# A fused attention, soft mixture and two-layer kernel: four kinds of vector work of a head pair take other places in its 18 half steps

## The chip, the cores and the metric

The kernel runs on one core of a Trainium2 chip. The metric is the device time of one execution in microseconds (us). Three executions of the kernel before took 703.08, 703.65 and 704.19 us, median 703.65.

## What is computed

The reference has three stages in a row, all in float32:

```python
q_pool = q.reshape(B, H, S // 2, 2, D).mean(axis=3)      # B 4, H 8, S 1152, D 64
attn = softmax(q_pool @ k^T / sqrt(D))
x = (attn @ v)  ->  (B * S / 2, H * D) = (2304, 512)
logits = x @ phi;  dispatch softmax over tokens, 8 experts of 4 slots, relu, combine softmax over slots
h = x @ w_in;  g = h (h >= 1), 0 (h <= -1), (h + 1)^2 / 4 between;  out = g @ w_out
```

Only the first stage, the attention, is touched by the change. It takes about the first 408 us.

## The kernel before

**Pairs, steps and half steps.** The 32 heads are handled as 16 pairs P = 0 to 15, two heads of one batch at a time, so a batch is four pairs. A pair is 9 steps, one for each chunk of 128 keys, and a step has two halves, one for each head. A half step is called a slot here: slot s of a pair is step s // 2, half s % 2, and runs from 0 to 17. Slot 18 is slot 0 of the next pair. The loop over all steps is at L694, and for each half it emits, in this order: one half of a maximum for the pair that comes 11 steps later (L711), the scores of this chunk (`st`, L373), the products with V of the step before (`pv`, L404), and then whatever the tables have put into this slot (`slot`, L619).

**The maximum.** The row maximum that the softmax subtracts is taken as max(a, b) = relu(a - b) + b over the two halves of the keys. In an even slot the matmuls multiply the queries with the difference of the key halves (`KD`) and ScalarE takes the relu (L332). In an odd slot the matmuls multiply with the first half of the keys and one VectorE instruction adds, and reduces to a maximum (L335, called the reduce here).

**The three score buffers.** All these matmul results and the scores share one pool of three PSUM tiles (L70, L72), taken in turn: maximum of slot s, scores of slot s, maximum of slot s + 1, scores of slot s + 1 and so on. With three tiles the scores of slot s + 1 take the tile that the maximum of slot s had. So the scores of an even slot can start only when the reduce of the odd slot before has ended, and the scores of an odd slot only when the relu of the even slot before has ended.

**Sums of exponentials.** ScalarE takes the exponential of each score tile (L388). VectorE adds the tiles of chunks 1 to 7 to a running sum for each head (`es_add`, L391; table `ADD`, entries (slot, chunk, head)). TensorE reduces the sums at the start of the next pair (`es_sum`, L396), where it also transposes the output of an earlier pair and takes its logits (`t_x`, L435).

**Preparing a pair.** Some 24 steps before a pair starts, its keys and queries are loaded (`load_k` L236, `load_q` L244). ScalarE then makes the high parts of the keys in float16 (`prep_khi`, L262, one for each head), VectorE the low parts (`prep_klo`, L267), both go through a DMA transpose (`xpose_k`, L276), and VectorE takes the difference of the key halves (`k_diff`, L313). For the queries VectorE adds neighbours (`prep_qp`, L282), ScalarE makes the high part (`prep_qhi`, L288), a DMA transposes it (`xpose_q1`, L299), VectorE makes the low part (`prep_qlo`, L295). The buffers of the raw keys, the raw queries and the high and low parts (`kf`, `qf`, `kn`) are there once, so each load waits for the last use by the pair before.

**Where each piece goes.** `plan` (L567) puts all this into slots, from the tables `PREP` and `KDS` (L37, L38; half steps relative to the start of the pair; -37 is 19 steps before it, second half) and `ADD` (L32). One table of `PREP` is for pair 2, the other for pairs 3 to 15. In a slot the pieces come in the order of pairs, and behind them the weight conversion: `cv_abs` on ScalarE and four VectorE steps (`cv_step`, L207), one weight block in each pair, from the table `CVS` (L26; first the slot of `cv_abs`, then of the four steps). VectorE, ScalarE and the queue that issues all DMAs (SP) each run their instructions in the order in which they were emitted.

A pair P is prepared while pair P - 2 runs, so what the tables set for pair 10 is seen in the slots of pair 8. In the middle of the attention pair 8 starts at 226.87 us and pair 6 at 177.21 us, counted at their first scores.

Of the kernel before, what the change touches and what calls it, by code (L numbers as in the profile page):

```python
# [22 lines left out]
MB = {1: 3, 2: 10, 3: 20}  # L23
DU = (3, 4, 5)

CVS = (10, 12, 17, 18, 19), (8, 9, 10, 11, 12)  # L26
CVL = 1
P1G = 0, 1, 1, 2, 2, 3, 4, 5, 6
TML = (3, 0, 4), (6, 1, 4)
WPH = 6  # L30

ADD = (((4, 1, 0), (4, 1, 1), (6, 2, 0), (8, 2, 1), (9, 3, 0), (8, 3, 1), (11, 4, 0),  # L32
        (10, 4, 1), (11, 5, 0), (14, 5, 1), (16, 6, 0), (14, 6, 1), (17, 7, 0), (17, 7, 1)),
       tuple((2 * c + h + 1 + (c < 8), c, h) for c in range(1, 9) for h in range(2)))
ADD += tuple((16, *x[1:]) if x == (17, 7, 0) else x for x in ADD[0]),

PREP = (-20, (-36, -35), (-34, -33), (-33, -32), -33, -32, -31, -30), (-24, (-42, -40), (-37, -37), (-35, -34), -38, -37, -35, -31)  # L37
KDS = -26, -19  # L38


@with_exitstack
def fused_kernel(ctx: ExitStack, tc: tile.TileContext, q, k, v, phi, w1, w2, w_in, w_out, out):
# [521 lines left out]
    def at(g, slot, f, *a):  # L564
        sched.setdefault((g, slot), []).append((f, a))

    def plan(P):  # L567
        b = NK * P
        if P > 1:
            lk, hk, lok, xk, aq, hq_, xq, loq = PREP[P > 2]  # L570

            def sl(x, f, *a):
                at(b + x // 2, x % 2, f, *a)

            for h in range(2):
                at(b + lk, h, (load_k2, load_q)[h], P)
                sl(hk[h], prep_khi, P, h)
                sl(lok[h], prep_klo, P, h)
                sl(xk[h], xpose_k, P, h)
                sl(KDS[h], k_diff, P, h)  # L580
            sl(aq, prep_qp, P)
            sl(hq_, prep_qhi, P)
            sl(xq, xpose_q1, P)
            sl(loq, prep_qlo, P)
            sl(xq + (6 if P > 2 else 4), dup_q1, P)
        if P > 0:
            at(b - 8, 1, load_v, P)
            at(b - 4, 0, s2_fill, P, 0, 5)
            at(b, 0, s2_fill, P, 5, NK)
        last = P == NP - 1  # L590
        for s, *a in ADD[2 if P in (5, 9, 13) else last]:
            at(b + s // 2, s % 2, es_add, P, *a)
        if not last:
            pre.setdefault((b + 9, 0), []).append((es_sum, P))
        q_ = P // HPB
        if last:
            at(b + 9, 0, t_raw, P, 0)
            at(b + 9, 1, t_raw, P, 1)
            for f, *a in ((es_sum, P), (t_sum, P, 0), (t_sum, P, 1), (t_fin, P), (t_x, P, True), (warm, WARM[0]), (t_last, P),
                          (lg_mx, q_), (lg_tr, q_), (warm, WARM[5]), (lg_max, q_), (lg_rep, q_), (p_old, q_), (warm, WARM[1]), (lg_exp, q_),  # L600
                          (p_mm, q_), (warm, WARM[6]), (p_add, q_)):
                at(b + 10, 0, f, *a)
            return
        g0 = b + (11 if P == NP - 2 else 18)
        pre.setdefault((g0, 0), []).insert(0, (t_x, P))
        for i in range(2):
            at(g0, 0, t_ev, P, i)
        at(b + 10, 0, t_fin, P)
        for c, h, t in TML:
            at(g0 + c // 2, c % 2, t_mul, P, h, t)  # L610
        at(g0 + 3, 1, lg_add, P)
        for h in range(2):
            at(b + 9, h, t_raw, P, h)
            at(b + 9, h, t_sum, P, h)
        if P % HPB == HPB - 1:
            for s, f, *a in ((10, lg_mx), (12, lg_tr), (12, lg_max), (14, lg_rep), (14, lg_exp), (16, p_mm), (16, p_add)):
                late.setdefault((g0 + s // 2, s % 2), []).append((f, (q_, *a)))
# [11 lines left out]
    with tc.manual_schedule():  # L629
# [51 lines left out]
        for P in range(NP):  # L681
            plan(P)
        g1_ = NK * (NP - 1)
        for n in range(16):
            ab, *st_ = [2 * NK * n + x for x in CVS[n // 15]]
            at(*divmod(ab, 2), cv_abs, n)
# [7 lines left out]
        for g in range(-LEAD, nsteps + 1):  # L694
            mx = [divmod(g + LEAD, NK)] if not NK <= g + LEAD < 2 * NK else []
            mx += [(1, t) for t in range(NK) if P1G[t] == g]
            P, c = divmod(g, NK)
# [489 lines left out]
```

## Time and profile before

| | |
|---|---|
| median of 3 runs | 703.65 us |
| the profiled execution | 703.25 us, span 701.4 us |
| TensorE (PE) busy | 690.0 us, 98% |
| VectorE (DVE) busy | 556.4 us, 79%; slices of 99% in most of the attention |
| ScalarE (ACT) busy | 497.5 us, 71% |
| granted TensorE clock | 1.00 throughout |
| mean DMA share of q1 | 61.9% over the span |

The profile is one execution, and times in it are counted from the start of its span. The busy share of TensorE counts a matmul from its start to a modelled end, and matmuls overlap, so how far TensorE is held up is read from the starts of its matmuls instead. A timeline row gives start, duration, engine, line, operation, tiles and count, and in brackets idle time before it.

### The profile page before, as it was taken

To read this page: it belongs to the slowest core of one execution; us is meant where nothing else is said; L and a number is where in the kernel's file an instruction comes from. 1 tells how busy PE (TensorE), PEld (TensorE's weight loads), DVE (VectorE), ACT (ScalarE), POOL (GpSimd) and SP (SyncE) were. 2 spreads that over 40 slices of the span, in tenths; PEclk is the share of its full clock that TensorE was granted. 3 is DMA by queue.
4 is the path that set the end of the run, shared out by engine and by line. 5 is a ranking of instruction groups with operands and counts; after the bars stand their busy time and mean duration, and the time that the engine had idled before them with its cause. 6 is when DMAs were issued, how large, how long until landed. Compare 5 with 4: busy or idle time off the path is not lost.

```text
span 701.4 us, 18916 instructions
## 1 busy us (share of the span) xinstructions
PE 690.0 (98%) x7639; PEld 548.1 (78%) x7639; DVE 556.4 (79%) x1094; ACT 497.5 (71%) x884; POOL 139.4 (20%) x123
## 2 busy tenths in 40 slices
PE   8899999999999999999999999999999999999997
PEld 8678878887888887888887876348888888888886
DVE  5699999999899999999998867327678888796542
ACT  4688888788788887788886865118787686677640
POOL 5100110110110110110010020113444353345340
PEclk9999999999999999999999999999999999999999
DMA  9978789988888987987885567993002212200222
GB/s 210 232 159 217 166 214 232 229 174 237 206 171 243 228 165 215 227 173 212 227 202 162 166 220 279 413 383 111 1 31 91 71 50 76 77 30 1 90 90 91
DMA packets 133766, 118.70 MB, mean 169 GB/s; under 512 B 81392, under 2 KB 103920, under 8 KB 131632
## 3 DMA queue, kind: packets, MB, share of 16 engines
q1 hardware_dynamic: 133680, 117.50, 61.9%
q8 instruction: 60, 0.98, 0.6%
q14 instruction: 26, 0.21, 0.1%
HBM read 82.90 MB, written 8.91 MB: 131 GB/s over the span
## 4 chain that ended last, share of the span: by engine, by line
PE 91%; DVE 4%; DMA 2%; ACT 1%; issue 1%; SPq 0%; POOL 0%; DVEq 0%; POOLq 0%; ACTq 0%
PE po L1023 27%; PE st L383 20%; PE acc L408 19%; PE mx L325 10%; PE h L953 2%; PE acc L401 2%; PE h L766 2%; DVE RW L335 2%; PE fill L344 2%; PE ty L448 1%; DMA Wst<-cv_dr 1%; PE tx L442 1%; PE s2o L823 1%; PE pb L537 1%; DVE es L394 0%
## 5 line engine op out<-in xcount | busy, mean ns | idle before, releaser
L388 ACT ACTIVATE e<-st 128x576 f32<-128x576 f32 x288 | 187.5, 652 | 53.0 <-PE st L383 51.9
L408 PE MATMUL acc<-e,vf 128*64 128x288 f32 x1152 | 198.4, 406 | 0.2 <-ACT e L388 0.2
L394 DVE TENSOR_TENSOR es<-es,e 128x576 f32<-128x576 f32 x194 | 144.4, 758 | 5.7 <-ACT e L388 0.4
L383 PE MATMUL st<-q,K 128*64 128x288 f16 x1152 | 129.5, 287 | 2.0 <-ACT e L388 0.5
L383 PE MATMUL st<-q,S 128*64 128x288 f16 x1152 | 129.5, 286 | 0.0
L335 DVE CUSTOM_DVE_ANT_0 RW<-mx,RW 128x576 f32<-128x576 f32 x144 | 108.4, 755 | 23.8 <-ACT e L388 14.2
L325 PEld LDWEIGHTS <-q 128*64 128x64 f16 x1152 | 74.3, 110 | 55.6 <-issue 8.4
L1023 PE MATMUL po<-whi,ghi 128*128 128x512 f32 x280 | 109.3, 390 | 0.0
L1023 PE MATMUL po<-wlo,ghi 128*128 128x512 f32 x280 | 109.0, 389 | 0.0
L1023 PE MATMUL po<-whi,glo 128*128 128x512 f32 x280 | 108.6, 388 | 0.0
L992 POOL TENSOR_TENSOR glo<-r,ghi 128x1024 fp32r<-128x1024 f32 x34 | 81.9, 2408 | 112.6 <-DVE r L980 66.3
L332 ACT ACTIVATE RW<-mx 128x576 f32<-128x576 f32 x144 | 93.4, 650 | 14.2 <-PE mx L325 9.5
L408 PEld LDWEIGHTS acc<-e,vf 128*64 128x64 f32 x1152 | 84.2, 137 | 2.1 <-ACT e L388 1.2
L383 PEld LDWEIGHTS <-K 128*64 128x64 f16 x1152 | 75.8, 109 | 11.7 <-issue 7.8
L489 POOL TENSOR_TENSOR xl<-xl,ss 128x320 f32<-128x320 f32 x15 | 12.5, 830 | 363.3 <-DVE wst L214 192.4
L383 PEld LDWEIGHTS <-S 128*64 128x64 f16 x1152 | 76.3, 110 | 1.0
L1035 DVE TENSOR_TENSOR pa<-po,pa 128x512 f32<-128x512 f32 (+1 forms) x54 | 36.8, 682 | 38.5 <-PE po L1023 38.4
L325 PE MATMUL mx<-KD,q 128*64 128x288 f16 x576 | 62.4, 287 | 3.1 <-DMA q<-qn 1.4
L325 PE MATMUL mx<-K,q 128*64 128x288 f16 x576 | 62.7, 288 | 0.1
L1023 PEld LDWEIGHTS po<-whi,glo 128*128 128x128 f32 x280 | 52.6, 188 | 11.4 <-POOL glo L992 0.3
L1023 PEld LDWEIGHTS po<-whi,ghi 128*128 128x128 f32 x280 | 52.7, 188 | 10.4 <-issue 0.4
L1023 PEld LDWEIGHTS po<-wlo,ghi 128*128 128x128 f32 x280 | 52.7, 188 | 9.5
(205 smaller groups left out, 900.6 us busy)
## 6 DMA issues: line engine op xcount, KB each, us to landing
w<-in_moe_w_dram SPq DMA_DIRECT2D x76, 256.0 KB, 4.0
w<-in_moe_w_dram SPq DMA_DIRECT2D x12, 1024.0 KB, 10.8
vf<-in_v_dram SPq DMA_DIRECT2D x16, 576.0 KB, 5.9
kf<-in_k_dram SPq DMA_DIRECT2D x30, 288.0 KB, 6.9
f<-in_moe_w_in_dram SPq DMA_DIRECT2D x16, 512.0 KB, 5.2
f<-in_moe_w_out_dram SPq DMA_DIRECT2D x16, 512.0 KB, 3.5
qf<-in_q_dram SPq DMA_DIRECT2D x30, 256.0 KB, 7.7
out_dram<-pa SPq DMA_DIRECT2D x17, 256.0 KB, 2.0
```

The lines of the kernel that those rows point to most:

```text
L325: nc.tensor.matmul(ps[p0:p1, i, 0:HQ], lhsT=q1[P][:, t, p0:p1], rhs=kk[:, i * HQ:(i + 1) * HQ], start=True, stop=True)
L332: nc.scalar.activation(out=RW[:, t % 2], in_=ps[:, :, 0:HQ], func=AF.Relu)
L335: nc.vector.tensor_tensor_reduce(out=r, in0=ps[:, :, 0:HQ], in1=r, scale=1.0, scalar=-3.0e38, op0=ALU.add, op1=ALU.max, accum_out=mp[P][:, ...
L344: nc.tensor.matmul(fl[0][:, 0:128], lhsT=ident, rhs=ident, start=True, stop=True)
L383: nc.tensor.matmul(ps[c0:c0 + 64, i, 0:HQ], lhsT=kk[:, ci, c0:c0 + 64], rhs=f[:, sl[i]], start=first, stop=not first)
L388: nc.scalar.activation(out=e, in_=ps[:, :, 0:HQ], func=AF.Exp, scale=ESC)
L394: nc.vector.tensor_tensor(out=Es[P, h], in0=E[P, 0, h] if c == 1 else Es[P, h], in1=E[P, c, h], op=ALU.add)
L401: nc.tensor.matmul(acc[P, h][32 * r:32 * r + 32, HQ:HQ + SW], lhsT=ones.to_broadcast([128, 32]), rhs=a, start=False, stop=False, skip_grou ...
L408: nc.tensor.matmul(acc[P, i][h * 64:(h + 1) * 64, 0:HQ], lhsT=vt[P][:, h, c, :], rhs=E[P, c, h][:, i, :], start=(c == 0), stop=(c == NK - ...
L992: nc.gpsimd.tensor_tensor(out=glo[k], in0=r, in1=ghi[k].bitcast(F32), op=ALU.subtract)
L1023: nc.tensor.matmul(ps, lhsT=a, rhs=b, start=st_, stop=sp)
L1035: nc.vector.tensor_tensor(out=t, in0=po, in1=t, op=ALU.add)
```

## The change

For pairs 3 to 15 the loads of keys and queries move one step later (-24 to -23), the two high parts one half step later, the two low parts from one slot (-37) to two (-33 and -30), their transposes from -35 and -34 to -32 and -29, the addition of queries one half step earlier (-38 to -39), and the second key difference from -19 to -16. In all pairs but the last, four additions move: (chunk 5, head 0) from slot 11 to 12, (5, 1) from 14 to 13, (6, 0) from 16 to 14, (7, 0) from 17 to 16. The last already stood at 16 in pairs 5, 9 and 13, whose own table goes away. The second conversion step moves from slot 17 to 16. No instruction is added or removed.

```diff
-CVS = (10, 12, 17, 18, 19), (8, 9, 10, 11, 12)
+CVS = (10, 12, 16, 18, 19), (8, 9, 10, 11, 12)
 ADD = (((4, 1, 0), (4, 1, 1), (6, 2, 0), (8, 2, 1), (9, 3, 0), (8, 3, 1), (11, 4, 0),
-        (10, 4, 1), (11, 5, 0), (14, 5, 1), (16, 6, 0), (14, 6, 1), (17, 7, 0), (17, 7, 1)),
+        (10, 4, 1), (12, 5, 0), (13, 5, 1), (14, 6, 0), (14, 6, 1), (16, 7, 0), (17, 7, 1)),
        tuple((2 * c + h + 1 + (c < 8), c, h) for c in range(1, 9) for h in range(2)))
-ADD += tuple((16, *x[1:]) if x == (17, 7, 0) else x for x in ADD[0]),
-PREP = (...), (-24, (-42, -40), (-37, -37), (-35, -34), -38, -37, -35, -31)
-KDS = -26, -19
+PREP = (...), (-23, (-41, -39), (-33, -30), (-32, -29), -39, -37, -35, -31)
+KDS = (-26, -19), (-26, -16)
...
-                sl(KDS[h], k_diff, P, h)
+                sl(KDS[P > 2][h], k_diff, P, h)
...
-        for s, *a in ADD[2 if P in (5, 9, 13) else last]:
+        for s, *a in ADD[last]:
```

The entries of `PREP` are: loads (a step), high parts, low parts, key transposes (each for two heads), query addition, query high part, query transpose, query low part.

Seen in the slots of a running pair, the vector work stands so (the reduce of each odd slot comes first in it):

| slots | before | after |
|---|---|---|
| 1, 2 | conversion step 4; end of the pair before (L431, L433) | the same, key difference 1 |
| 3, 4 | two additions | low part, two additions |
| 5, 6 | query low part, addition | query low part, addition, low part |
| 7, 8 | two additions | the same |
| 9, 10 | two additions, key difference 0 | the same |
| 11, 12 | two additions, conversion step 1 | the same order |
| 13, 14 | L348, two additions | L348, three additions |
| 15, 16 | addition, query addition | query addition, addition, conversion step 2 |
| 17, 18 | two additions, key difference 1, two low parts, conversion step 2, L463, conversion step 3 | addition, L463, conversion step 3 |

## Rows read from the trace of the kernel before

**Rows 1.** The page: busy time of each engine, and the chain that ended last.

```profile
PE 690.0 (98%) x7639; PEld 548.1 (78%) x7639; DVE 556.4 (79%) x1094; ACT 497.5 (71%) x884; POOL 139.4 (20%) x123
...
PE 91%; DVE 4%; DMA 2%; ACT 1%; issue 1%; SPq 0%; POOL 0%; DVEq 0%; POOLq 0%; ACTq 0%
```

**Rows 2.** Busy time by stretch: pairs 6 and 8, first score to first score (length first).

```profile
177.21:201.98 24.77, 24.77 (x366) 20.47 (x367) 22.44 (x46) 20.63 (x38) 2.54 (x3) 1.00 0.88 192
...
226.87:251.76 24.89, 24.79 (x370) 20.53 (x367) 23.30 (x47) 20.84 (x39) 2.12 (x3) 1.00 0.90 212
```

**Rows 3.** Timeline of TensorE, pair 8: slots 1 to 3, then slots 13 and 14.

```profile
230.71 0.41 PE L383 MATMUL st<-q,K 128*64 128x288 f16 x4
...
232.19 0.44 PE L383 MATMUL st<-q,K 128*64 128x288 f16 x4
...
233.41 0.44 PE L383 MATMUL st<-q,K 128*64 128x288 f16 x4
...
245.61 0.44 PE L383 MATMUL st<-q,K 128*64 128x288 f16 x4
...
246.88 0.44 PE L383 MATMUL st<-q,K 128*64 128x288 f16 x4
```

**Rows 4.** Timeline of VectorE from slot 17 of pair 7 to slot 1 of pair 8.

```profile
225.99 0.76 DVE L335 CUSTOM_DVE_ANT_0 RW<-mx,RW 128x576 f32<-128x576 f32 x1 [0.31 <-ACT e L388]
...
226.67 1.42 DVE L394 TENSOR_TENSOR es<-es,e 128x576 f32<-128x576 f32 x2
228.01 0.45 DVE L315 TENSOR_TENSOR KD<-K 128x576 f16<-128x576 f16 x1
228.38 1.42 DVE L273 SCALAR_TENSOR_TENSOR kn<-kf,kn 128x576 f16<-128x576 f32 x2
229.72 0.42 DVE L214 TENSOR_SCALAR wst<-wst 128x512 int32<-128x512 int32 x1
230.05 0.68 DVE L463 TENSOR_TENSOR xl<-tx,ss 128x512 f32<-128x512 f32 x1
...
231.39 0.75 DVE L335 CUSTOM_DVE_ANT_0 RW<-mx,RW 128x576 f32<-128x576 f32 x1
```

**Rows 5.** Timeline of VectorE in slots 13 to 15 of pair 8.

```profile
246.06 0.75 DVE L335 CUSTOM_DVE_ANT_0 RW<-mx,RW 128x576 f32<-128x576 f32 x1
...
246.94 1.61 DVE L394 TENSOR_TENSOR es<-es,e 128x576 f32<-128x576 f32 x2
248.47 0.75 DVE L335 CUSTOM_DVE_ANT_0 RW<-mx,RW 128x576 f32<-128x576 f32 x1
```

**Rows 6.** Timelines of VectorE, TensorE and ScalarE in slots 1 to 3 of pair 6.

```profile
181.37 0.76 DVE L335 CUSTOM_DVE_ANT_0 RW<-mx,RW 128x576 f32<-128x576 f32 x1 [0.35 <-ACT es L427]
...
183.81 0.76 DVE L335 CUSTOM_DVE_ANT_0 RW<-mx,RW 128x576 f32<-128x576 f32 x1
...
182.27 0.41 PE L383 MATMUL st<-q,K 128*64 128x288 f16 x4
...
183.64 0.44 PE L383 MATMUL st<-q,K 128*64 128x288 f16 x4
...
182.92 0.66 ACT L332 ACTIVATE RW<-mx 128x576 f32<-128x576 f32 x1
```

**Rows 7.** Loads of keys and queries: times to landing, and who waited (L242, L253).

```profile
DMA to landing us min/median/max: 2.9/6.9/8.5
...
DMA to landing us min/median/max: 3.3/5.8/6.9
```

**Rows 8.** Timeline of SyncE: the issues of a key transpose and of loads, pair 8.

```profile
232.69 1.53 SPq L279 DMA_TRANSPOSE K<-kn  x1
...
235.94 0.90 SPq L242 DMA_DIRECT2D kf<-in_k_dram  x2
```

**Rows 9.** Line 220 (conversion step 4), the two groups, and GpSimd in pair 8.

```profile
L220 DVE SCALAR_TENSOR_TENSOR wst<-f,wst x16: 684/931/942, 55.8 to 423.6; 128x512 int32<-128x512 int32 x16
...
230.99 1.45 POOL L496 TENSOR_TENSOR xT<-xT,xl 128x160 f32<-128x160 f32 x2
```

More of the change, by code (lines that the diff above doesn't have):

```diff
@@ L32 @@
 ADD = (((4, 1, 0), (4, 1, 1), (6, 2, 0), (8, 2, 1), (9, 3, 0), (8, 3, 1), (11, 4, 0),
-        (10, 4, 1), (11, 5, 0), (14, 5, 1), (16, 6, 0), (14, 6, 1), (17, 7, 0), (17, 7, 1)),
+        (10, 4, 1), (12, 5, 0), (13, 5, 1), (14, 6, 0), (14, 6, 1), (16, 7, 0), (17, 7, 1)),
        tuple((2 * c + h + 1 + (c < 8), c, h) for c in range(1, 9) for h in range(2)))
-ADD += tuple((16, *x[1:]) if x == (17, 7, 0) else x for x in ADD[0]),
-PREP = (-20, (-36, -35), (-34, -33), (-33, -32), -33, -32, -31, -30), (-24, (-42, -40), (-37, -37), (-35, -34), -38, -37, -35, -31)
-KDS = -26, -19
+PREP = (-20, (-36, -35), (-34, -33), (-33, -32), -33, -32, -31, -30), (-23, (-41, -39), (-33, -30), (-32, -29), -39, -37, -35, -31)
+KDS = (-26, -19), (-26, -16)
 @with_exitstack
```

## The prediction

> **What bounds the kernel now.** I read the page first: TensorE is busy 98% of the span, and 91% of the chain that ended last is TensorE's [rows 1]. That says little yet, since a matmul that waits for the next to start still counts. So I went to the starts of the scores. In the middle of the attention one slot follows the other after 1.22 us, a step after 2.44 us: 232.19 to 233.41 [rows 3]. Slot 1 of pair 8 takes 1.48 us (230.71 to 232.19), 0.26 more, and slot 13 takes 1.27 (245.61 to 246.88), 0.05 more [rows 3]. Nothing else in that pair is late, so of its 24.89 us [rows 2] some 24.58 are TensorE's own work and 0.31 are lost. That is all a better order could give back in a plain pair.
>
> Who makes TensorE late is seen in VectorE's timeline. The scores of slot 2 start at 232.19, right when the reduce of slot 1 (231.39, 0.75 long) ends at 232.14 [rows 3, 4]: they take its PSUM tile. On time, the reduce would have begun 0.36 us earlier, at 231.03 (0.59 us behind its matmuls, as in the slots where VectorE had idled before; slot 1 of pair 6 is such a one, idle 0.35 [rows 6]). So 0.36 late cost 0.26; in slot 13 0.11 late cost 0.05. A reduce may thus be about 0.08 us late for nothing, and everything over that is TensorE's loss. After the loss the whole pace has shifted, and only those 0.08 are carried on. This is the rule of my sum: **each step has one deadline, and between two reduces there is 2.44 us of VectorE time.**
>
> **Prices.** From start to start, a reduce takes 0.68 (225.99 to 226.67), an addition 0.67 (two in 1.34, 226.67 to 228.01), the key difference 0.37, a low part 0.67 (two in 1.34), conversion step 2 0.33, all in [rows 4]. Two additions to the same sum in a row take 1.53 (246.94 to 248.47 [rows 5]), as the second waits for the first. A query addition and a query low part have the same shape as an addition, and I take 0.67 for each too. From reduce 13 to the first addition after it 0.88 pass (246.06 to 246.94 [rows 5]), L348 included.
>
> **What the change takes away.** At the end of a pair VectorE has two additions, a key difference, two low parts and the conversion step, 226.67 to 230.05, before L463 can start [rows 4]. One addition, the difference, both low parts and the step leave: 0.67 + 0.37 + 1.34 + 0.33 = 2.71. The 0.36 of slot 1 is gone. But slot 0 is also the one place where VectorE has room: TensorE takes 3.84 us for it (226.87 [rows 2] to 230.71 [rows 3]), 2.62 more than for another, on transposes, logits and sums. From reduce 17 to reduce 1 there are 2.44 + 2.62 = 5.06 us, and what is left to do is 0.68 + 0.67 + 1.34 (L463 and conversion step 3, 230.05 to 231.39 [rows 4]). L463 needs the transposes, so nothing moves up: VectorE will idle 2.37 us there.
>
> **What it adds, window by window** (a window runs from one reduce to the next; 2.44 is free, 0.08 grace, used up once):
> - Slots 1 to 3. Pair 6 is what a pair looks like whose slot 1 is on time: its slot 2 takes 1.37 (182.27 to 183.64 [rows 6]), 0.15 lost to ScalarE, whose relu (182.92 to 183.58 [rows 6]) comes late behind the last sums of the pair before. That stays. Its reduces stand 2.44 apart (181.37, 183.81 [rows 6]), with nothing left. The key difference adds 0.37: reduce 3 at 184.18, its end at 184.94, scores 0.14 late beyond the 0.15. Loss 0.29.
> - Slots 3 to 5: reduce, low part, two additions: 0.68 + 3 x 0.67 = 2.69, 0.25 over. Loss 0.25.
> - Slots 5 to 7: reduce, query low part, addition, low part: 2.69. Loss 0.25.
> - Slots 7 to 11: unchanged, and 0.2 of room in the first; the grace is back.
> - Slots 11 to 13: (5, 0) moves a slot, yet VectorE's order is the same. The 0.05 stays.
> - Slots 13 to 15: 0.88 and three additions, 2.01, make 2.89 (they alternate between the sums, so none waits): 0.45 over, and 0.01 from the window before. Loss 0.46. The high parts now stand in odd slots, ahead of a relu instead of behind an exponential. That makes the relu of slots 14 and 16 some 0.4 late, as in slot 2 of pair 6, worth 0.15; but TensorE already waits there for the reduce, so I add nothing. With that cover gone it is 0.15 twice.
> - Slots 15 to 17: 0.68 + 0.67 + 0.67 + 0.33 = 2.35, fits.
>
> The sum is 0.29 + 0.25 + 0.25 + 0.05 + 0.46 = 1.30 a pair in place of 0.31: **+0.99**. VectorE's total agrees: it was busy 23.30 of 24.89 us [rows 2], the work is nearly the same, and 2.37 us of idleness at the boundary with some 0.2 in slots 7 to 9 make a pair of 25.9.
>
> **Over all pairs.** Plain ones (2, 3, 4, 7, 8, 11, 12, like pair 8): 7 x 0.99 = 6.9. Pairs 6 and 10, which lose 0.19 now (24.77 [rows 2]): 2 x 1.11 = 2.2. Pairs 5, 9, 13, in which a batch is closed and which already had (7, 0) at 16: the first windows +0.05, 0.25 and 0.25, slots 13 to 15 +0.40, so 3 x 0.95 = 2.9. Pair 14 prepares nothing and has no reduce after slot 13: +0.1. Pair 0 has only slots 13 to 15: +0.4. Pair 1 lacks the moved difference: 0.25 + 0.25 + 0.46 - 0.31, +0.6. Together 13.1 us. The profiled execution took 703.25 us, 0.40 under the median; on the median the sum is 703.65 + 13.1 = **716.8 us**.
>
> **The queue of transfers.** SP issues in order. By the windows above, on pair 8's clock, reduce 1 stands at 231.03, reduce 3 at 233.84, reduce 5 at 236.53, reduce 13 near 246.6 and reduce 15 near 249.5. The second key transpose now waits for a low part that ends at 236.53 + 0.68 + 3 x 0.67 + 0.1, 239.3, and takes 1.53 to issue [rows 8]; behind it stand the copy of the queries, the loads of the next keys (0.45 each [rows 8]) and queries, and the copy of the scores' second operand. So keys are issued near 241.3 in place of 235.94 [rows 8], and the last queries near 244.5 (an estimate, with 0.5 to 0.6 an issue). Landing takes 2.9 to 8.5 us for keys and 3.3 to 6.9 for the last queries [rows 7], depending on what is ahead. Keys are needed near 247.5 (high part, behind the exponential of slot 13) and land between 244.2 and 249.8; queries are needed at 249.5 + 0.68, 250.2 (addition, slot 15), and land between 247.8 and 251.4. The wait is therefore 0 to 1.2 for queries, 0 to 2.3 for keys. I take 0 for both, because the large values of today come from loads issued in one burst behind others, and the new order spreads them; at the medians, 248.2 and 250.3, the waits would be 0.7 and 0.1, and I keep that as a rival. The cover of the moved loads is these 5 to 6 us. The copy behind them (needed in slot 0 of the next pair) has 7. GpSimd's queue is passed by nothing that moves.
>
> **A rule weighed against a row.** Conversion step 4 takes 0.68 at the least and 0.93 at the median; it is long where GpSimd's additions, until 232.44, run beside it [rows 9]. So company costs 0.25, and it does so already. After the change the step starts at 231.71 in place of 232.06, deeper in that company; the moved difference and low part start after 233, behind it. I add nothing. The Trainium skill, "SBUF — State Buffer", section "Who interferes with whom", says that a VectorE instruction with two SBUF inputs and a GpSimd instruction that reads SBUF exclude each other and that the loser blocks fully. The row's 0.25 is less than that; rival 4 is what full blocking would do.
>
> **Rivals.**
> 1. **Late loads on top** (chance 0.14). A wait for keys or queries of 0.7 to 1.2 comes in 13 preparing pairs and little of it is covered: 716.8 + 13 x 0.7 to 13 x 1.1, 726 to 731. For it: today's landing times. Against it: the burst ahead of the loads is gone.
> 2. **Faster** (0.06). The stall in slot 1 goes and the full windows are absorbed, because a reduce may be 0.45 late for nothing in place of 0.08 (that is the point from which it decides): 7 x 0.26 gained, 701.8. Slot 13 speaks against it: 0.11 late already cost 0.05.
> 3. **Only part of it** (0.09). Mixed instructions follow closer than equal ones, each 0.67 being 0.60: the windows of 2.69 lose 0.05 in place of 0.25, slots 13 to 15 lose 0.25, a pair 0.69: +0.38 in place of 0.99, 709.
> 4. **GpSimd blocks VectorE** (0.03). Conversion step 4 is held until GpSimd is done at 232.44, 0.73 behind its start in place of 0.25: 0.48 more in 13 pairs, 723. The rule above would have it so.
> 5. **No change** (0.03): VectorE's order is not what the tables say. In the rows of before it follows them exactly.
>
> The forecast, 712 to 721, has 0.65. The range for 8 in 10 takes in rivals 3 and 4 and the near end of rival 1, and leaves out 0.19: 709 to 727. The three runs differ by 0.16%, so 0.2% (1.4 us) is about what can be told from no change. Faster 0.06; within it 0.04, rival 5 and a bit; slower 0.90.
>
> **What would show it.** After the change the rows of a plain pair should give: 25.9 us a pair; slot 1 at 1.22 us; 1.4 to 1.5 us from score to score in slots 2, 3, 5 and 7, and slots 14 and 15 together 0.46 longer than 2.44; VectorE idle over 2 us before L463 and the reduce of slot 1, and hardly anywhere else. I am wrong if slots 3 to 7 keep 1.22 although VectorE has three pieces between reduces, or if VectorE's idle time names a DMA before L286 or ScalarE's before L265 (rival 1).

## The result and the profile after

The changed kernel takes 714.06 us (median of 4, 713.75 to 714.66) where the kernel before takes 703.92 (4 runs): **1.0149, 95% interval 1.0136 to 1.0161, 10.1 us slower**. The forecast was 716.8 (709 to 727).

The page of the changed kernel: TensorE's busy share is 98% as before [rows 1], while its part of the chain that ended last fell from 91% to 75% and VectorE's rose from 4% to 16%.

```profile
PE 699.0 (98%) x7639; PEld 547.7 (77%) x7639; DVE 551.0 (77%) x1094; ACT 496.8 (70%) x884; POOL 135.7 (19%) x123
...
PE 75%; DVE 16%; ACT 4%; issue 3%; DMA 1%; DVEq 0%; POOL 0%; ACTq 0%; POOLq 0%
```

The same pairs by stretch (length first, then busy time of TensorE, weight loads, VectorE). Pair 8 went from 24.89 to 25.79, pair 6 from 24.77 to 25.72 [rows 2]; VectorE's busy time in pair 8 even fell, from 23.30 to 22.98.

```profile
181.23:206.95 25.72, 25.48 (x365) 20.37 (x366) 22.85 (x47) 20.64 (x38) 1.87 (x3) 1.00 0.73 198
232.74:258.53 25.79, 25.55 (x369) 20.38 (x366) 22.98 (x47) 20.84 (x39) 1.79 (x3) 1.00 0.82 206
```

TensorE's timeline of pair 8, the starts of the scores of slots 1 to 8 and 13 to 17 (compare [rows 3]; line numbers are one lower than before):

```profile
236.58 0.41 PE L382 MATMUL st<-q,K 128*64 128x288 f16 x4
237.80 0.41 PE L382 MATMUL st<-q,K 128*64 128x288 f16 x4
239.17 0.44 PE L382 MATMUL st<-q,K 128*64 128x288 f16 x4
240.49 0.44 PE L382 MATMUL st<-q,K 128*64 128x288 f16 x4
241.70 0.44 PE L382 MATMUL st<-q,K 128*64 128x288 f16 x4
243.17 0.44 PE L382 MATMUL st<-q,K 128*64 128x288 f16 x4
244.38 0.44 PE L382 MATMUL st<-q,K 128*64 128x288 f16 x4
245.85 0.44 PE L382 MATMUL st<-q,K 128*64 128x288 f16 x4
...
251.95 0.44 PE L382 MATMUL st<-q,K 128*64 128x288 f16 x4
253.22 0.44 PE L382 MATMUL st<-q,K 128*64 128x288 f16 x4
254.54 0.44 PE L382 MATMUL st<-q,K 128*64 128x288 f16 x4
256.09 0.44 PE L382 MATMUL st<-q,K 128*64 128x288 f16 x4
257.31 0.44 PE L382 MATMUL st<-q,K 128*64 128x288 f16 x4
```

Taking each from the next and comparing with 1.22 gives what each slot loses:

| slots of pair 8 | lost before | forecast | lost after |
|---|---|---|---|
| 1 | 0.26 | 0 | 0.00 |
| 2 and 3 | 0 | 0.29 | 0.15 + 0.10 |
| 5 | 0 | 0.25 | 0.25 |
| 7 | 0 | 0.25 | 0.25 |
| 13 | 0.05 | 0.05 | 0.05 |
| 14 and 15 | 0 | 0.46 | 0.10 + 0.33 |
| sum | 0.31 | 1.30 | 1.23 |

VectorE's timeline of the same pair shows both sides of the change. At the end of the pair it now idles, 1.24 us before L462 and 1.08 before the reduce of slot 1, 2.32 in all (forecast 2.37). From reduce 1 to reduce 3 it takes 2.78 us (236.90 to 239.68; forecast 2.44 + 0.37 = 2.81). In the full windows behind, nothing is idle: from reduce 3 to reduce 5 it is 2.68 us (239.68 to 242.36), from 5 to 7 2.68, from 13 to 15 2.88 (252.40 to 255.28), where 2.44 are free (compare [rows 4, 5]).

```profile
234.53 0.69 DVE L462 TENSOR_TENSOR xl<-tx,ss 128x512 f32<-128x512 f32 x1 [1.24 <-PE tx L441]
235.14 0.68 DVE L216 SCALAR_TENSOR_TENSOR wst<-f,wst 128x512 int32<-128x512 int32 x1
236.90 0.76 DVE L334 CUSTOM_DVE_ANT_0 RW<-mx,RW 128x576 f32<-128x576 f32 x1 [1.08 <-ACT es L426]
...
239.68 0.75 DVE L334 CUSTOM_DVE_ANT_0 RW<-mx,RW 128x576 f32<-128x576 f32 x1
...
242.36 0.75 DVE L334 CUSTOM_DVE_ANT_0 RW<-mx,RW 128x576 f32<-128x576 f32 x1
...
245.04 0.75 DVE L334 CUSTOM_DVE_ANT_0 RW<-mx,RW 128x576 f32<-128x576 f32 x1
...
252.40 0.75 DVE L334 CUSTOM_DVE_ANT_0 RW<-mx,RW 128x576 f32<-128x576 f32 x1
...
253.28 2.09 DVE L393 TENSOR_TENSOR es<-es,e 128x576 f32<-128x576 f32 x3
255.28 0.75 DVE L334 CUSTOM_DVE_ANT_0 RW<-mx,RW 128x576 f32<-128x576 f32 x1
```

The loads, issued a step later, did not become late: keys (L241, first line) and the last queries (L252) now land sooner after their issue than before, 3.5 for 6.9 and 3.8 for 5.8 at the median [rows 7]. From 30 us of the span to the end of the attention, no idle time over 0.03 us of ScalarE or VectorE ends with the landing of a transfer.

```profile
DMA to landing us min/median/max: 2.9/3.5/5.3
...
DMA to landing us min/median/max: 3.0/3.8/5.6
```

### The profile page after: what moved, and what is told of

Same layout as the page of the kernel before. It is cut to its first block, busy times and chain, and to the rows that moved or that the text cites. A ratio compares the mean times of both kernels' runs of the same rounds, so it can differ in the third digit from the quotient of the medians.

```text
span 712.6 us, 18941 instructions
## 1 busy us (share of the span) xinstructions
PE 699.0 (98%) x7639; PEld 547.7 (77%) x7639; DVE 551.0 (77%) x1094; ACT 496.8 (70%) x884; POOL 135.7 (19%) x123
## 4 chain that ended last, share of the span: by engine, by line
PE 75%; DVE 16%; ACT 4%; issue 3%; DMA 1%; DVEq 0%; POOL 0%; ACTq 0%; POOLq 0%
PE po L1022 27%; PE st L382 14%; PE acc L407 11%; DVE RW L334 6%; PE mx L324 6%; DVE es L393 4%; PE acc L400 2%; PE h L952 2%; PE s2o L822 2%; PE h L765 2%; PE fill L343 2%; DVE kn L272 2%; PE ty L447 1%; ACT e L387 1%; DVE qn L295 1%
## 5 line engine op out<-in xcount | busy, mean ns | idle before, releaser
L393 DVE TENSOR_TENSOR es<-es,e 128x576 f32<-128x576 f32 x194 | 142.6, 757 | 3.7 <-ACT e L387 0.4
L1022 PEld LDWEIGHTS po<-whi,glo 128*128 128x128 f32 x280 | 52.6, 188 | 11.4 <-POOL glo L991 0.3
```

Of the source, the lines that this page charges most:

```text
L393: nc.vector.tensor_tensor(out=Es[P, h], in0=E[P, 0, h] if c == 1 else Es[P, h], in1=E[P, c, h], op=ALU.add)
L1022: nc.tensor.matmul(ps, lhsT=a, rhs=b, start=st_, stop=sp)
```

## The experiments

### Parts of the change undone, one at a time

**Low parts back** (the changed kernel, only this edit):

```diff
-PREP = (...), (-23, (-41, -39), (-33, -30), (-32, -29), -39, -37, -35, -31)
+PREP = (...), (-23, (-41, -39), (-37, -37), (-35, -34), -39, -37, -35, -31)
```

> The changed kernel with the low parts of keys and their two transposes back at the end of a pair (-37, -37 and -35, -34). If each step's VectorE work is what sets the loss (window theory), slots 5 and 7 of a plain pair go from 1.47 back to 1.22 us, the end of the pair (0.68 + 0.67 + 1.34 + 1.34 = 4.03 of 5.06 us) still fits, so slot 1 stays at 1.22, and 12 pairs give back 0.50 and one 0.25: about 6.2 us, 707.9. If instead the lengthening of slots 5 and 7 came from the later loads or from ScalarE's high parts, both unchanged here, the time stays at 714.

Measured: 708.92 us, ratio to the kernel before 1.0080 (95% interval 1.0065 to 1.0095). Each ratio is taken to runs of the kernel before that were measured beside the variant; here their median is 703.58. The scores of slots 5 to 8 of pair 8:

```profile
238.81 0.44 PE L382 MATMUL st<-q,K 128*64 128x288 f16 x4
240.03 0.44 PE L382 MATMUL st<-q,K 128*64 128x288 f16 x4
241.25 0.44 PE L382 MATMUL st<-q,K 128*64 128x288 f16 x4
242.47 0.44 PE L382 MATMUL st<-q,K 128*64 128x288 f16 x4
```

All 1.22 apart: the two low parts are the whole loss of slots 5 and 7, half the slowdown. From the first scores of pair 0 to those of pair 15 the profile shows 6.0 us less than the changed kernel's (384.43 for 390.48), as expected; the time of the whole kernel fell by 5.1. Loads and ScalarE's high parts were still where the change puts them, so it is not their doing.

**Additions and the conversion step back** (the tables `ADD` and `CVS` of before, without the separate table for pairs 5, 9, 13):

```diff
-CVS = (10, 12, 16, 18, 19), ...
+CVS = (10, 12, 17, 18, 19), ...
-        (10, 4, 1), (12, 5, 0), (13, 5, 1), (14, 6, 0), (14, 6, 1), (16, 7, 0), (17, 7, 1)),
+        (10, 4, 1), (11, 5, 0), (14, 5, 1), (16, 6, 0), (14, 6, 1), (17, 7, 0), (17, 7, 1)),
```

> The changed kernel with the four additions and the conversion step back in their old slots. VectorE's window from slot 13 to 15 falls from 2.89 to 2.41 us, so its loss of 0.44 in slots 14 and 15 goes. Theory A: ScalarE's moved high parts then show by themselves, slots 14 and 16 keep 0.11 to 0.15 each, and 14 pairs give back 0.2: 711.3. Theory B: only VectorE counts, slots 14 to 16 all go to 1.22: 714.1 - 14 x 0.44 = 707.9.

Measured: 712.46 us, 1.0130 (1.0115 to 1.0145): theory A, though less was given back than its 711.3. The scores of slots 13 to 17 of pair 7:

```profile
225.23 0.44 PE L382 MATMUL st<-q,K 128*64 128x288 f16 x4
226.49 0.44 PE L382 MATMUL st<-q,K 128*64 128x288 f16 x4
227.82 0.44 PE L382 MATMUL st<-q,K 128*64 128x288 f16 x4
229.04 0.44 PE L382 MATMUL st<-q,K 128*64 128x288 f16 x4
230.36 0.44 PE L382 MATMUL st<-q,K 128*64 128x288 f16 x4
```

Slot 15 is back at 1.22, while slots 14 (1.33) and 16 (1.32) now lose 0.11 and 0.10 to ScalarE: the moved high part (L264) runs between an exponential and the relu, which is then late. In pairs 4 and 8 of this profile slot 3 takes 1.63 and 1.67 where the changed kernel has 1.32, which is part of the shortfall; why, wasn't followed up. ScalarE in slots 13 and 14:

```profile
226.01 0.65 ACT L387 ACTIVATE e<-st 128x576 f32<-128x576 f32 x1 [0.57 <-PE st L382]
226.56 0.68 ACT L264 ACTIVATE kn<-kf 128x576 f16<-128x576 f32 x1
227.13 0.64 ACT L331 ACTIVATE RW<-mx 128x576 f32<-128x576 f32 x1
```

**Loads and high parts back:**

```diff
-PREP = (...), (-23, (-41, -39), (-33, -30), (-32, -29), -39, -37, -35, -31)
+PREP = (...), (-24, (-42, -40), (-33, -30), (-32, -29), -39, -37, -35, -31)
```

> The changed kernel with loads and high parts back (loads at -24, high parts at -42 and -40). Window theory: slot 14 loses its 0.11 and slot 15 takes it (0.33 becomes 0.44), since the reduce of slot 15 is late by the same amount: no change, 714. If ScalarE's lateness adds to VectorE's, or the loads cost something, 13 pairs give back 0.11: 712.6 or less.

Measured: 714.73 us, 1.0160 (1.0145 to 1.0175), no different from the changed kernel. In pair 8 slot 14 is back at 1.22 (253.66 to 254.88) and slot 15 takes 1.66 (254.88 to 256.54):

```profile
253.66 0.44 PE L382 MATMUL st<-q,K 128*64 128x288 f16 x4
254.88 0.44 PE L382 MATMUL st<-q,K 128*64 128x288 f16 x4
256.54 0.44 PE L382 MATMUL st<-q,K 128*64 128x288 f16 x4 [0.25 <-DVE mp L334]
```

The loss stays whole, 0.44 in one slot in place of 0.10 + 0.33 in two. ScalarE's lateness was covered by VectorE's, and the loads cost nothing where they are. (Their tables went back a whole step, their issue by 2.0 us: keys went out at 245.60, 12.4 us behind the start of pair 8, in place of 14.4.)

**Key difference back:**

```diff
-KDS = (-26, -19), (-26, -16)
+KDS = (-26, -19), (-26, -19)
```

> The changed kernel with the second key difference back at -19 for all pairs. Window theory: slot 3 goes from 1.32 to 1.22 in the nine pairs where it is 1.32 and by 0.03 in four others, the end of the pair keeps room (3.06 of 5.06 us): about 1.0 us less, 713.1. If slot 2's 0.15 were the difference's doing as well, 0.25 in 12 pairs, 3 us: 711.1.

Measured: 711.07 us, 1.0110 (1.0093 to 1.0127), 3 us less and not 1. The number is that of the other branch, but its mechanism isn't: slot 2 keeps its 0.15. The scores of slots 2 to 6 of pair 8:

```profile
236.38 0.41 PE L382 MATMUL st<-q,K 128*64 128x288 f16 x4
237.74 0.44 PE L382 MATMUL st<-q,K 128*64 128x288 f16 x4
238.96 0.44 PE L382 MATMUL st<-q,K 128*64 128x288 f16 x4
240.18 0.44 PE L382 MATMUL st<-q,K 128*64 128x288 f16 x4
241.44 0.44 PE L382 MATMUL st<-q,K 128*64 128x288 f16 x4
```

Slot 3 gave back its 0.10, and slot 5 went from 1.47 to 1.26. So the 0.15 that ScalarE costs in slot 2 isn't a cost beside VectorE's: while TensorE waits for the relu, VectorE gains those 0.15 on its next deadline. With the difference in the window that gain was used up at once; without it, it lasts until slot 5. The difference costs 0.3 in pair 8 (25.79 for 25.50), most of the 0.37 it was priced at, and not the 0.10 that slot 3 shows.

### Low parts alone, in the kernel before

```diff
-PREP = (...), (-24, (-42, -40), (-37, -37), (-35, -34), -38, -37, -35, -31)
+PREP = (...), (-24, (-42, -40), (-33, -30), (-32, -29), -38, -37, -35, -31)
```

> The kernel before with only the low parts of keys and their transposes moved (-33, -30 and -32, -29). Window theory: VectorE's work at the end of a pair falls from 5.40 to 4.06 of 5.06 us, so slot 1 loses its 0.26 and slot 2 shows 0.15 of ScalarE instead; slots 5 and 7 take 0.25 each: +0.39 in a plain pair (7), +0.5 in pairs 6 and 10, +0.4 in 5, 9 and 13: about 5 us, 709. If relieving the end of the pair were worth more than the filled windows, under 703.9.

Measured: 706.53 us, 1.0034 (1.0022 to 1.0046), about half of what was expected, for the same reason: in most plain pairs slots 2, 5 and 7 lose 0.15, 0.04 and 0.25 (expected: 0.15, 0.25 and 0.25). Slower all the same, although slot 1 is at 1.22 there. In pairs 4, 6 and 12 of this profile slots 1, 3 or 5 lost 0.15 to 0.27 more; why, wasn't followed up.

### Can the end of the pair be relieved for nothing?

The windows of slots 11 to 17 had a little room, so a version better than both seemed possible.

**One conversion step moved, in the kernel before:**

```diff
-CVS = (10, 12, 17, 18, 19), (8, 9, 10, 11, 12)
+CVS = (10, 12, 16, 18, 19), (8, 9, 10, 11, 12)
```

> The kernel before with only the conversion step moved from slot 17 to 16. Window theory: the end of a pair has 5.07 of 5.06 us, slots 15 to 17 have 2.35 of 2.44; slot 1 goes from 1.48 to about 1.22 and slot 2 from 1.22 to 1.37: 0.11 less in some ten pairs, 702.8. If a VectorE window needs more slack than that, no change or a new loss at slot 17: 704 or more.

Measured: 703.30 us, 0.9991 (0.9982 to 0.9999), and slot 1 of pair 8 still takes 1.48, where 1.22 was expected. VectorE did reach L463 sooner, 1.75 us behind the start of TensorE's transposes (229.12) in place of 2.08, yet the reduce of slot 1 starts 3.42 us behind them as before. VectorE at the start of pair 8:

```profile
230.87 0.68 DVE L463 TENSOR_TENSOR xl<-tx,ss 128x512 f32<-128x512 f32 x1
231.47 1.15 DVE L217 SCALAR_TENSOR_TENSOR wst<-f,wst 128x512 int32<-128x512 int32 x1
232.54 0.74 DVE L335 CUSTOM_DVE_ANT_0 RW<-mx,RW 128x576 f32<-128x576 f32 x1
```

Between them conversion step 3 (L217) takes 1.15 us. GpSimd's first addition runs beside it:

```profile
231.33 0.74 POOL L489 TENSOR_TENSOR xl<-xl,ss 128x320 f32<-128x320 f32 x1 [22.16 <-ACT xl L460]
```

In the kernel before, the same two at the start of pair 8 (between the rows of [rows 4]); the step took 0.81:

```profile
230.65 0.81 DVE L217 SCALAR_TENSOR_TENSOR wst<-f,wst 128x512 int32<-128x512 int32 x1
...
230.18 0.74 POOL L489 TENSOR_TENSOR xl<-xl,ss 128x320 f32<-128x320 f32 x1 [22.61 <-DVE wst L214]
```

**Two conversion steps moved**, the first between the two additions of slots 11 and 12:

```diff
-CVS = (10, 12, 17, 18, 19), (8, 9, 10, 11, 12)
+CVS = (10, 11, 16, 18, 19), (8, 9, 10, 11, 12)
-        (10, 4, 1), (11, 5, 0), ...
+        (10, 4, 1), (12, 5, 0), ...
```

> As the conversion step alone, and the first conversion step placed between the two additions of slots 11 and 12, so that the second addition no longer waits for the first. Window theory: the window from slot 11 to 13 falls from 2.55 to 2.35 us, slot 13 goes from 1.27 to 1.22: 0.16 less in plain pairs, 0.05 in pairs 6 and 10: about 1.6 us under the kernel before, 702.3. Rival: the addition waits for its predecessor all the same, slot 13 stays, 702.8.

Measured: 702.63 us, 0.9980 (0.9971 to 0.9989). Slot 13 went to 1.22 as expected; slot 1 stayed at 1.48, as in the run before.

**Conversion step 3 ahead of GpSimd**, on top of that:

```diff
-CVS = (10, 11, 16, 18, 19), (8, 9, 10, 11, 12)
+CVS = (10, 11, 16, 17, 19), (8, 9, 10, 11, 12)
```

> As the kernel with two conversion steps moved, and conversion step 3 (L217) one slot earlier as well, so that VectorE runs it ahead of L463 and before GpSimd's additions start. Theory after the last runs: L217 took 1.15 us and ended no sooner when it was reached sooner, since GpSimd's addition beside it held it; ahead of it the step takes 0.68, slot 1 of a plain pair goes from 1.48 to 1.22, and slot 2 shows ScalarE's 0.15: 0.11 less in ten pairs, 1 us under that kernel, 701.6. Rival: the end of the pair is simply too full (5.0 of 5.06 us): slot 1 keeps 1.4 or more, 702.6.

Measured: 701.99 us, 0.9980 (0.9972 to 0.9989); the runs of the kernel before that were measured beside it have a median of 703.35, those beside the variant with two steps moved 703.80. The intervals of the two variants overlap; what shows the mechanism is the trace. From the first scores of pair 0 to those of pair 15 this one takes 377.35 us, the other 378.29. L217 starts 0.46 before GpSimd's addition (229.00 against 229.46) and takes 0.69, the reduce of slot 1 stands at 230.31, and slot 1 of pairs 2 to 14 takes 1.22. VectorE at the start of pair 8, and GpSimd's first addition:

```profile
229.00 0.69 DVE L217 SCALAR_TENSOR_TENSOR wst<-f,wst 128x512 int32<-128x512 int32 x1
229.60 0.69 DVE L463 TENSOR_TENSOR xl<-tx,ss 128x512 f32<-128x512 f32 x1
230.31 0.76 DVE L335 CUSTOM_DVE_ANT_0 RW<-mx,RW 128x576 f32<-128x576 f32 x1
...
229.46 0.83 POOL L489 TENSOR_TENSOR xl<-xl,ss 128x320 f32<-128x320 f32 x1 [22.70 <-ACT xl L460]
```

**ScalarE's second sum one slot earlier**, first as the last piece of slot 0 (on the kernel with two steps moved), then as the first piece (on the kernel just shown):

```diff
+        at(b + 9, 0, t_sum, P, 1)
         for h in range(2):
             at(b + 9, h, t_raw, P, h)
-            at(b + 9, h, t_sum, P, h)
+        at(b + 9, 0, t_sum, P, 0)
```

> As the kernel with two conversion steps moved, and ScalarE's second sum (L427) one slot earlier, in slot 0, where ScalarE waits. If slot 2's 0.15 is ScalarE's relu held up by 0.27 us of that sum, slot 2 goes to 1.22 as well and a plain pair loses nothing of its 0.31: about 3.5 us under the kernel before, 700.4. If the relu is held up by the copy alone, or the sum waits for TensorE in slot 0, 702.3 or more.

As the last piece: 703.56 us, 0.9994 (0.9985 to 1.0003), no gain where 700.4 was expected. In pairs 6 and 10 slot 2 went to 1.22, but slot 1 to 1.41: the products of slot 1 write the PSUM tile that the sum reads, and waited for it, 0.3 us in pair 6. The loss moved; pair 6 took 24.77 as in the kernel before. In the plain pairs slot 1 stayed near 1.48. In this profile keys also came late once: ScalarE waited 0.74 us for them in pair 2, whose slot 13 took 2.20.

> As the kernel before it in this list, and ScalarE's second sum (L427) moved to slot 0 ahead of the copy and the first sum there. Theory: pv of slot 1 no longer waits for it (it did, by 0.2, where the sum stood last in slot 0), and the relu of slot 2 is no longer late: slots 1, 2 and 13 of a plain pair all take 1.22, 24.58 us a pair, 0.15 less in 13 pairs: 2 us under h1, 699.7 to 700. Rival: TensorE's products wait for the sums in slot 0 or the relu stays late for the copy alone: no better than h1.

As the first piece: **699.69 us, 0.9955 (0.9941 to 0.9968), faster than both kernels.** Slots 1, 2 and 13 of pair 8 all take 1.22. In pair 8 no slot but slot 0 is longer than 1.22, and by stretch (length first) it takes 24.56:

```profile
225.17:249.73 24.56, 24.56 (x369) 19.01 (x366) 23.38 (x47) 20.83 (x39) 1.88 (x3) 1.00 0.88 214
```

## Why the prediction was right

**The forecast mechanism is shown.** The reduce of each odd slot is a deadline, VectorE's pieces between two reduces follow each other at their pitch, and what exceeds 2.44 us is lost one for one. Slots 5 and 7 were forecast at 0.25 and measured at 0.25; slots 14 and 15 together were forecast at 0.46 and measured at 0.43, VectorE's idle time at the end of a pair forecast at 2.37 and measured at 2.32. Undoing each part changed the slots of its own window, and those behind it only where time gained is carried on. The half step that the query addition moved wasn't undone by itself; slot 16, behind its new window, takes 1.22 in the changed kernel.

**The queue of transfers** was rightly taken at 0. The time of issue was right: keys were forecast 14.4 us behind the start of pair 8 (241.3 against 226.87) and went out 14.4 behind it (247.14 against 232.74). They land sooner, and it is the new place of the low parts and their transposes that decides this, not the later loads: with these alone put back, keys take 6.2 us to land at the median again, with loads and high parts alone put back 3.4. That fits the burst named in the prediction. In the kernel before, loads of 512 and 576 KB and a copy were issued at 234.31, 234.99 and 235.43, right ahead of the keys (235.94); in the changed kernel the two loads go out at 238.57 and 238.99, over 8 us ahead of the keys (247.14). Rival 1 falls: from 30 us on neither ScalarE nor VectorE waited for a load, and the run with the loads back is no faster.

**ScalarE's high parts** were rightly taken as covered: back in place they change nothing in the sum, and with the cover gone they cost 0.11 and 0.10 (0.15 was put on each).

**What was off is the size**: 13.1 us forecast, 10.1 between the medians. From the first scores of pair 0 to those of pair 15 the two profiles differ by 11.4 us (390.48 and 379.09). The two profiled executions differ by 11.1 (714.34 and 703.25), as one lies 0.3 above its median and the other 0.7 below. The 11.4 come out lower than the 13.1 in three terms:
- Plain pairs other than pair 2 grew by 0.90 to 1.01 us, pair 8 by 0.90, for the 0.99 of the sum; pairs 6 and 10 by 0.95 for 1.11. The term that was too large is slots 1 to 3: it was 0.25 in place of 0.29, and 0.18 in pairs 6 and 10. I put the difference's whole 0.37 on top of 2.44, but the window from reduce 1 to reduce 3 became 2.78 in pair 8 and 2.70 in pair 6 (185.39 to 188.09). The pieces don't simply add up there, since L430 waits for ScalarE's sum (L426): in pair 6 VectorE idles 0.20 before it (0.31 before the change).
- Pairs 0, 1 and 2 together: +1.3 for 2.0, for the most part since they lost more before than pair 8, from which I took the base: pair 0 0.26 in slot 13, pair 1 0.43 in slots 1 and 3, pair 2 0.48 in slots 1 and 13.
- Pairs 5, 9 and 13: 0.82 to 0.89 each for 0.95.

**One step of the reasoning was wrong without harm.** I read slot 1's 0.36 as VectorE's queue alone. Shortening that queue by 0.33 did nothing for it, and putting conversion step 3 ahead of GpSimd's addition removed it. In the kernel before, the addition lengthened the step by 0.13 (0.81 for 0.68), the queue did the rest; with the shorter queue the step ran into the addition sooner and was held longer. The change itself took 2.71 us out of this window, so that VectorE was through at 235.82 (235.14, 0.68 long) before GpSimd began at 236.05, and the forecast for that slot held. I hadn't looked at this, so that part is luck.

**Rival 4** was right on the blocking and wrong on the price. Conversion step 4 of pair 8 starts 0.40 us before GpSimd's additions end (237.59 and 237.99), not the 0.73 that the rival took from the old times, because the last of them starts some 0.3 sooner against the pair. The step takes 0.95, as before (0.94).

## What to carry to other kernels

Where an engine has one deadline in each step, sum its work between deadlines, not over the pair: spare time in one long window can't be spent in the full ones, and moving work out of the long window costs up to its whole duration in the full ones. Two engines that are late for the same consumer can share their loss: undo one alone and the other appears, so price parts together. Before moving work off a late piece, see whether that piece itself is held by something beside it: a duration that grows when it starts sooner is a wait.

## What the runs showed of the hardware

A VectorE instruction with two SBUF inputs that starts while a GpSimd addition runs is held until that addition is done. Conversion step 3 took 0.69 us when it started first (step 3 ahead of GpSimd), 0.81 when it started 0.27 before the end of GpSimd's addition (kernel before), and 1.15 when it started 0.60 before that end (one conversion step moved: 231.47, while the addition ended at 232.07). Its end stayed where it was: 0.54 behind GpSimd's end in the second case, 0.55 in the third. In pairs 3 to 13 of these three profiles and of the changed kernel's, every conversion step 3 or 4 that starts behind such an addition ends 0.54 to 0.56 behind it. Conversion step 4 of pair 8 in the kernel before is one, where it ends at 233.00, 0.56 behind GpSimd's additions (232.44 [rows 9]):

```profile
232.06 0.94 DVE L220 SCALAR_TENSOR_TENSOR wst<-f,wst 128x512 int32<-128x512 int32 x1
```

It goes the other way too. In pair 6 of the kernel before, conversion step 3 starts first (180.34, 0.68 long), and GpSimd's addition, started at 180.51, takes 1.10 in place of the 0.74 of pair 8.

The Trainium skill, "SBUF — State Buffer", section "Who interferes with whom", says that a VectorE instruction with two SBUF inputs contends with a GpSimd instruction that reads SBUF, that the port pair they share is an exclusive lock, and that the order of issue decides who blocks. These rows agree, but for 0.13 us: a held step ends 0.55 behind GpSimd, not the 0.68 that it takes alone. My prediction held the page against L220's 0.25 and concluded that the trace shows less than the page. That was a misreading: L220 started only 0.38 us before GpSimd's end, so being held until then accounts for the 0.25 (0.38 less 0.13).
